# One kernel of attention, experts and feed-forward: the rare-case branch moves from the middle to the end, the mask limits come in one transfer, and TensorE gets more filler work at the start

## The chip, the cores and the metric

One NeuronCore of one Trainium2 chip. The time is that of one execution on the device, in microseconds. Before the change the median of 3 runs is 661.46 us (661.29 to 661.57). All inputs are fp32; the outputs are fp32 too.

## What is computed

Three layers in a row, on 2 x 768 = 1536 tokens of 512 features:

```
attention (8 heads of 64): each query sees the first n_sink = 4 keys and the last window = 128 keys
x   = softmax(q k^T / 8, masked) v                          # 1536 x 512
experts (8, of 512 -> 1024 -> 512), one per token:
e   = argmax(cos(x, expert_emb) / tau);  g = its softmax weight
x   = g * relu(x @ w1[e]) @ w2[e]
feed-forward (512 -> 1536 -> 512):
out = ((x @ w_a) * (x @ w_b)) @ w_out
```

n_sink, window and the split of tokens over experts are data: the kernel must be right for any values, and is laid out for the likely ones.

## The kernel before

Every large product is made of three TensorE products of rounded parts (hi x hi, lo x hi, hi x lo), so each operand is first split into `hi` (a cast on ScalarE, ACT) and `lo` (a difference on VectorE, DVE). Each engine runs its instructions in the order in which they are written (`manual_schedule`); semaphores keep the dependencies.

**Attention.** 12 blocks of 128 queries, four steps each (`g` counts them), software-pipelined: in step g TensorE makes the transposes of step g-2 (`p_t`), the score products of step g (`sc_mm`), the value products of step g-3 (`pv`) and some products that prepare the choice of expert (`back`). DVE adds the mask and takes the maximum, ACT makes the exponentials. The masks are built on DVE by `early_masks` from `ctli`, which holds n_sink and window for each partition and is filled by two small DMAs on the queue of SyncE (SP), between the first and the second halves of the first q and k blocks. `warm_pe(n)` puts n transposes of the identity, of no use for the result, on TensorE: 15 before the loop and `WARMG[g]` at the end of step g.

**Experts.** Tokens are gathered by expert and worked off in single tiles and pairs of tiles, out of a list `seq` of 81 items; the position in it is `i`. Beside it `side_gen` makes, three small steps an item, the tables for putting tokens back in order: `cidx`, the row of `y_d` that each token of the last stage reads, and `cide`, the same for the first four tiles, limited to the rows that are written early. At fixed items the last stage is prepared: `load_conv` loads its weights (SP queue), `conv_abs`, `conv_b0`, `conv_b1` and `conv_step` unpack and split them, `gather_y` gathers rows of `y_d` (POOL), `y_t` and `y_s` transpose and split them. The expert results go to DRAM through ACT (`y_out`) and SP.

**The covering path.** The plan has room for the likely spread of tokens. `cnt` counts what doesn't fit, or says that the mask limits are unlikely ones. All engines read it into a register (L1473) and branch (L1475): if it is zero, which it is here, the whole body is skipped; else the missing rows are computed slowly, and `y_d` is rewritten. Behind the branch the feed-forward stage begins.

**Feed-forward.** Three groups (`gi`) of 512 tokens, in each 12 slices (`f`) of 128 hidden features. `ab_mms` makes 24 products (`pp`), `g_split` multiplies the two halves and splits the product (ACT, DVE, ACT, DVE), `out_mms` adds 12 products to `po` one slice later. In the first group the weights of slices 2 to 11 are still unpacked on the way, two `conv_step` a slice. At the end of a group `done` scales the four result tiles and POOL writes them to `out` by indirect DMA.

Of the kernel before, what the change touches and what calls it, by code (L numbers as in the profile page):

```python
# [20 lines left out]
P = 128  # L21
# [42 lines left out]
WARMG = [6, 3, 4, 1]  # L64
# [38 lines left out]
TINY = 2.0 ** -15 * 1.125  # L103

# [19 lines left out]
def tile_kernel(ctx, tc, q, k, v, n_sink, window, emb, tau, w1, w2, wc, out, dbg=None):  # L124
# [62 lines left out]
    tt = pc.tile([E, 1], F32, name="tt")  # L187
    q0, k0 = new_q(0, 0), new_k(0, 0)
    for a in (0, W2):
        ld(q0, q, 0, 0, a, a + W2)  # L190
        ld(k0, k, 0, 0, a, a + W2)
        if a == 0:
            nc.sync.dma_start(ctli[:, 0:2], n_sink.bitcast(I32).partition_broadcast(P))
            nc.sync.dma_start(ctli[:, 2:4], window.bitcast(I32).partition_broadcast(P))
# [976 lines left out]
    fe = pool(ctx, "fe", side="right")  # L1171

    def side_gen(w_, pl, psp, tag):
# [172 lines left out]
        V.tensor_copy(cide, cpos[:, 0:4])  # L1346
        G.tensor_scalar(g, g, 1.0 / GSC, None, op0=ALU.mult)
# [16 lines left out]
    wres = {}  # L1364

    raw2, sq2 = {}, {}
# [3 lines left out]
    def load_conv(m):  # L1370
        if m >= NH:
            return
        r = raw2[m] = fe.tile([P, HW, 2], I32, tag="raw", name="raw2", bufs=3)
        nc.sync.dma_start(r.rearrange("p n c -> p (n c)"), wc32[m])

    def conv_abs(m):
        if m < NH:
            sq2[m] = fe.tile([P, HW], F32, tag="sq", name="sq", bufs=2)
            nc.scalar.activation(sq2[m], raw2[m][:, :, 1].bitcast(F32), AF.Abs)  # L1379

    def conv_b0(m):
        if m < NH:
            b, t = sq2[m], sq2[m].bitcast(I32)
            nc.vector.tensor_scalar(b, b, TINY, None, op0=ALU.max)  # L1384
            nc.vector.tensor_scalar(t, t, 5, 2, op0=ALU.logical_shift_left, op1=ALU.logical_shift_right)

    def conv_b1(m):
        if m < NH:
            r, t = raw2.pop(m), sq2[m].bitcast(I32)
            nc.vector.scalar_tensor_tensor(t, r[:, :, 0], 29, t, op0=ALU.logical_shift_right, op1=ALU.bitwise_or)  # L1390
            nc.vector.scalar_tensor_tensor(t, r[:, :, 1], -1073741824, t, op0=ALU.bitwise_and, op1=ALU.bitwise_or)  # L1391

    def conv_step(m, wpool):
        f, h = divmod(m, 2)
        if h == 0:
            wres[f] = (wpool.tile([P, CW], F32R, name=f"wh{f}"), wpool.tile([P, CW], F32R, name=f"wl{f}"))
        wh, wl = (t[:, h * HW:(h + 1) * HW] for t in wres[f])
        sq = sq2.pop(m)
        nc.scalar.copy(wh, sq)
        conv_b0(m + 1)  # L1400
        nc.vector.tensor_tensor(out=wl, in0=sq, in1=wh, op=ALU.subtract)  # L1401
        conv_abs(m + 2)
        conv_b1(m + 1)
        load_conv(m + 4)

    xh2 = fe.tile([P, NP, TG], F32R, name="xh2")
    xl2 = fe.tile([P, NP, TG], F32R, name="xl2")
    ygs = {}

    def gather_y(u, w=None, rows=None):  # L1410
        ygs[u] = w.tile([P, DM], F32, tag="ygn", name="ygn", bufs=4) if w else fe.tile([P, DM], F32, tag="yg", name="yg", bufs=3)
        early = u < 4 and w is None
        nc.gpsimd.indirect_dma_start(out=ygs[u], out_offset=None, in_=y_d[0:rows or (YR0 if early else YR1), :],  # L1413
                                     in_offset=bass.IndirectOffsetOnAxis(ap=(cide if early else cidx)[:, u:u + 1], axis=0))

    def y_t(u, psp, tag):
        yp = psp.tile([P, NP, P], F32, tag=tag, name="yp2")
        for kc in range(NP):
            nc.tensor.transpose(yp[:, kc, :], ygs[u][:, kc * P:(kc + 1) * P], ident)  # L1419
        return yp  # L1420

    def y_s(u, yp):
        tt = u % 4
        ts_ = slice(tt * P, (tt + 1) * P)
        nc.scalar.copy(xh2[:, :, ts_], yp)
        nc.vector.tensor_tensor(out=xl2[:, :, ts_], in0=yp, in1=xh2[:, :, ts_], op=ALU.subtract)
# [46 lines left out]
    ns_v = nc.values_load(cnt[0:1, 0:1], min_val=0, max_val=4 * int(GENF))  # L1473
    mst.close()
    with tc.If(ns_v > 0):  # L1475
# [97 lines left out]
        with ExitStack() as gs:  # L1573
            xw = pool(gs, "xw3")
            xps = pool(gs, "xps3", space=PSUM)
            for u in range(NU):
                gather_y(u, xw, NBLK * P)
                nc.sync.dma_start(y2_d[u * P:(u + 1) * P, :], ygs[u])
            for u in range(NU):
                yc = xw.tile([P, DM], F32, tag="ygn", name="yc", bufs=4)  # L1580
                nc.sync.dma_start(yc, y2_d[u * P:(u + 1) * P, :])
                nc.sync.dma_start(y_d[u * P:(u + 1) * P, :], yc)
            nc.vector.tensor_copy(cidx, tok)
            for u in range(4):
                gather_y(u, xw, YR1)
                y_s(u, y_t(u, xps, "a"))

    f1 = pool(ctx, "f1")
    f2 = pool(ctx, "f2", bufs=2, side="right")
    fpa = pool(ctx, "fpa", bufs=2, space=PSUM)  # L1590
    fpo = pool(ctx, "fpo", space=PSUM)

    def ab_mms(f):
        wh, wl = wres[f]
        ab = []
        for n in range(2):
            pp = fpa.tile([P, TG], F32, tag="ab"[n], name="pp")
            for kc in range(NP):
                ws = slice(n * 512 + kc * P, n * 512 + (kc + 1) * P)
                nc.tensor.matmul(pp, lhsT=wh[:, ws], rhs=xh2[:, kc, :], start=(kc == 0), stop=False)  # L1600
                nc.tensor.matmul(pp, lhsT=wh[:, ws], rhs=xl2[:, kc, :], start=False, stop=False)  # L1601
                nc.tensor.matmul(pp, lhsT=wl[:, ws], rhs=xh2[:, kc, :], start=False, stop=(kc == NP - 1))  # L1602
            ab.append(pp)
        return ab

    def g_split(f, ab, el):
        asb = f2.tile([P, TG], F32, tag="asb", name="asb", bufs=1)
        nc.scalar.copy(asb, ab[0])  # L1608
        nc.vector.tensor_tensor(out=asb, in0=ab[1], in1=asb, op=ALU.mult)  # L1609
        gh = f2.tile([P, TG], F32R, tag="gh", name="gh", bufs=2)  # L1610
        gl = f2.tile([P, TG], F32R, tag="gl", name="gl", bufs=2)
        nc.scalar.copy(gh, asb)  # L1612
        EL[el].tensor_tensor(out=gl, in0=asb, in1=gh, op=ALU.subtract)  # L1613
        return f, gh, gl

    def out_mms(po, f, gh, gl, done=None, tts=range(4)):
        wh, wl = wres[f]
        for tt in tts:
            ts_ = slice(tt * P, (tt + 1) * P)
            nc.tensor.matmul(po[tt], lhsT=gh[:, ts_], rhs=wh[:, 1024:CW], start=(f == 0), stop=False, skip_group_check=True)  # L1620
            nc.tensor.matmul(po[tt], lhsT=gh[:, ts_], rhs=wl[:, 1024:CW], start=False, stop=False, skip_group_check=True)  # L1621
            nc.tensor.matmul(po[tt], lhsT=gl[:, ts_], rhs=wh[:, 1024:CW], start=False, stop=(f == NF - 1), skip_group_check=True)  # L1622
            if done is not None:
                done(tt)

    NG = NT // TG
    outs = []
    pend = None
    tail = []
    for gi in range(NG):  # L1630
        po = [fpo.tile([P, DM], F32, tag=f"po{tt}", name=f"po{tt}") for tt in range(4)]
        for f in range(NF):
            ab = ab_mms(f)
            more = gi == 0 and f + NF0 < NF
            if more:
                conv_step(2 * (f + NF0), f1)
            cur = g_split(f, ab, 'V')
            if more:
                conv_step(2 * (f + NF0) + 1, f1)
            u0 = 4 * (gi + 1)  # L1640
            if f == NF - 2 and gi + 1 < NG:
                for tt in range(3):
                    gather_y(u0 + tt)
            if f == NF - 1 and gi + 1 < NG:
                yps = [y_t(u0 + tt, fpa, "ab"[tt]) for tt in range(2)]
                gather_y(u0 + 3)
                for tt in range(2):
                    y_s(u0 + tt, yps[tt])
            if pend is not None:
                if gi == NG - 1 and f == NF - 1:  # L1650
                    out_mms(*pend, tts=range(3))
                    tail.append(pend)
                else:
                    out_mms(*pend)
            pend = (po, *cur)
        if gi + 1 < NG:
            yps = [y_t(u0 + tt, fpa, "ab"[tt - 2]) for tt in range(2, 4)]

        def done(tt, gi=gi, po=po):
            os_ = fe.tile([P, DM], F32, tag="yg", name="os_", bufs=3)  # L1660
            u = gi * 4 + tt
# [63 lines left out]
```

## Time and profile before

| | |
|---|---|
| median of 3 runs | 661.46 us (661.29 to 661.57) |
| the profiled execution, whole | 659.85 us |
| its span, first to last instruction | 658.0 us |
| mean granted TensorE clock | 0.977 |
| attention, experts, feed-forward, about | 0 to 125, 125 to 329, 335 to 654 us |

All rows are from one profiled execution. PE is TensorE's products, PEld its weight loads, DVE VectorE, ACT ScalarE, POOL GpSimd, SP SyncE; a q behind a name means the sequencer of the engine, with its register, branch and semaphore instructions. L12 is line 12 of the kernel. A product's duration includes its way through the array, so products in a row overlap; their pace is the distance of their starts. The granted clock is a share of full speed: 1.00 is 2.4 GHz, 0.50 is 1.2 GHz.

### The profile page before, as it was taken

What the parts mean: (1) busy time and instruction counts of PE and PEld (TensorE: products, weight loads), DVE (VectorE), ACT (ScalarE), POOL (GpSimd) and SP (SyncE); (2) the same over time, 40 slices, a digit from 0 to 9 for tenths busy, and PEclk for the clock granted to TensorE, in tenths of its full rate; (3) what the DMA queues carried; (4) which work ended last, traced back from release to release, by engine and by line L of the source; (5) the groups of instructions that cost most, each with busy time, mean ns of one, the idle gap of its engine ahead of it and who ended that gap; (6) DMA issues with size and microseconds to landing.
All of it is one profiled execution on the core that took longest, in us unless ns stands there. A gap on an engine that the chain in (4) does not pass through costs nothing. (4 is left out here: it accounts for less than half of the span.)

```text
span 658.0 us, 10420 instructions
## 1 busy us (share of the span) xinstructions
PE 628.6 (96%) x3665; PEld 515.4 (78%) x3665; DVE 396.4 (60%) x910; ACT 304.8 (46%) x581; POOL 122.2 (19%) x269
## 2 busy tenths in 40 slices
PE   8999999889999999998969999999999999999995
PEld 5777777779998989887858767678888888888884
DVE  5688878998888766798839999943111113111111
ACT  4678777667575657667524444422111113111111
POOL 7243345481042211020010000004000003000002
PEclk7699999989999999999979999999999999999999
DMA  4244325323787887587253454203000002000001
GB/s 144 85 160 130 130 81 191 147 76 134 254 289 273 269 280 267 180 304 253 86 177 134 154 186 150 96 17 114 0 1 0 1 0 81 0 1 1 0 1 64
DMA packets 25967, 80.77 MB, mean 123 GB/s; under 512 B 3560, under 2 KB 4072, under 8 KB 25904
## 3 DMA queue, kind: packets, MB, share of 16 engines
q1 hardware_dynamic: 22560, 69.23, 31.5%
q0 software_dynamic: 3344, 10.77, 4.8%
q8 instruction: 31, 0.51, 0.3%
q14 instruction: 32, 0.26, 0.1%
HBM read 81.82 MB, written 10.75 MB: 141 GB/s over the span
## 5 line engine op out<-in xcount | busy, mean ns | idle before, releaser
L1600 PE MATMUL pp<-xh,wh 128*128 128x512 f32 x288 | 114.5, 398 | 5.7 <-DVEq L1475 5.7
L1609 DVE TENSOR_TENSOR asb<-pp,asb 128x512 f32<-128x512 f32 x36 | 24.8, 689 | 151.5 <-PE pp L1602 151.5
L1601 PE MATMUL pp<-xl,wh 128*128 128x512 f32 x288 | 114.9, 399 | 0.0
L1602 PE MATMUL pp<-xh,wl 128*128 128x512 f32 x288 | 114.6, 398 | 0.0
L603 DVE TENSOR_TENSOR lo<-raw,hi 128x1024 fp32r<-128x1024 f32 x80 | 96.1, 1228 | 7.9 <-ACT hi L595 6.2
L595 ACT CAST hi<-raw 128x1024 fp32r<-128x1024 f32 x87 | 88.0, 1050 | 7.8 <-PE hp L708 4.1
L1600 PEld LDWEIGHTS pp<-xh,wh 128*128 128x128 f32 x288 | 54.7, 190 | 19.4 <-ACTq L1475 6.2
L1601 PEld LDWEIGHTS pp<-xl,wh 128*128 128x128 f32 x288 | 54.8, 190 | 13.1
L1602 PEld LDWEIGHTS pp<-xh,wl 128*128 128x128 f32 x288 | 54.8, 190 | 12.9
L1612 ACT CAST gh<-asb 128x512 fp32r<-128x512 f32 x36 | 22.3, 620 | 90.2 <-DVE asb L1609 87.4
L1608 ACT COPY asb<-pp 128x512 f32<-128x512 f32 x36 | 21.0, 583 | 89.6 <-PE pp L1602 89.5
L1620 PE MATMUL po<-wh,gh 128*128 128x512 f32 x144 | 57.9, 402 | 3.9 <-ACT gh L1612 3.9
L477 ACT ACTIVATE p<-st,mn 128x260 f32<-128x260 f32 (+1 forms) x96 | 46.6, 487 | 29.2 <-DVE mn L474 22.8
L1622 PE MATMUL po<-wh,gl 128*128 128x512 f32 x144 | 57.6, 400 | 0.0
L1621 PE MATMUL po<-wl,gh 128*128 128x512 f32 x144 | 56.8, 394 | 0.0
L1413 POOL DMA_INDIRECT yg<-y_d,cidx x8 | 8.3, 1040 | 215.6 <-PE yp L1419 187.3
L780 PE MATMUL hT<-pxh,hi 128*128 128x256 f32 x160 | 45.5, 285 | 0.0
L782 PE MATMUL hT<-pxh,lo 128*128 128x256 f32 x160 | 44.7, 280 | 0.0
L781 PE MATMUL hT<-pxl,hi 128*128 128x256 f32 x160 | 44.7, 279 | 0.0
L474 DVE CUSTOM_DVE_ANT_0 st<-sc,m 128x260 f32<-128x260 f32 (+1 forms) x96 | 35.0, 399 | 10.4 <-PE sc L465 5.1
L1379 ACT ACTIVATE sq<-raw 128x768 f32<-128x768 f32 x24 | 22.1, 923 | 39.4 <-DVE wl L1401 39.4
L1613 DVE TENSOR_TENSOR gl<-asb,gh 128x512 fp32r<-128x512 f32 x36 | 24.9, 692 | 24.8 <-ACT gh L1612 24.8
(344 smaller groups left out, 1335.1 us busy)
## 6 DMA issues: line engine op xcount, KB each, us to landing
raw<-in_moe_w_dram SPq DMA_DIRECT2D x88, 512.0 KB
raw<-in_moe_w_dram SPq DMA_DIRECT2D x24, 768.0 KB
y_d<-ys SPq DMA_DIRECT2D x16, 256.0 KB
vt<-in_v_dram SPq DMA_DIRECT2D x12, 256.0 KB
x_d<-xl SPq DMA_DIRECT2D x12, 256.0 KB
qt<-in_q_dram SPq DMA_DIRECT2D x11, 256.0 KB
kt<-in_k_dram SPq DMA_DIRECT2D x10, 256.0 KB
qt<-in_q_dram SPq DMA_DIRECT2D x2, 128.0 KB
```

The source lines that it names most:

```text
L477: nc.scalar.activation(p[:, j, 0:W], st[:, 0:W], AF.Exp, bias=z['mn'][:, h:h + 1], scale=-1.0, accum_out=z['sm'][:, h:h + 1])
L595: ER = {'A': lambda o, i: nc.scalar.copy(o, i), 'V': lambda o, i: nc.vector.tensor_copy(o, i), 'P': lambda o, i: nc.gpsimd.tensor_copy(o, i)}
L603: EL[elo].tensor_tensor(out=lo, in0=raws[g], in1=hi, op=ALU.subtract)
L780: nc.tensor.matmul(hT[:, c, :], lhsT=hi[:, ws], rhs=z['xh'][:, kc, :], start=(c == 0 and kc == 0), stop=False, skip_group_check=True)
L781: nc.tensor.matmul(hT[:, c, :], lhsT=hi[:, ws], rhs=z['xl'][:, kc, :], start=False, stop=False, skip_group_check=True)
L782: nc.tensor.matmul(hT[:, c, :], lhsT=lo[:, ws], rhs=z['xh'][:, kc, :], start=False, stop=(kc == NP - 1), skip_group_check=True)
L1600: nc.tensor.matmul(pp, lhsT=wh[:, ws], rhs=xh2[:, kc, :], start=(kc == 0), stop=False)
L1601: nc.tensor.matmul(pp, lhsT=wh[:, ws], rhs=xl2[:, kc, :], start=False, stop=False)
L1602: nc.tensor.matmul(pp, lhsT=wl[:, ws], rhs=xh2[:, kc, :], start=False, stop=(kc == NP - 1))
L1620: nc.tensor.matmul(po[tt], lhsT=gh[:, ts_], rhs=wh[:, 1024:CW], start=(f == 0), stop=False, skip_group_check=True)
L1621: nc.tensor.matmul(po[tt], lhsT=gh[:, ts_], rhs=wl[:, 1024:CW], start=False, stop=False, skip_group_check=True)
L1622: nc.tensor.matmul(po[tt], lhsT=gl[:, ts_], rhs=wh[:, 1024:CW], start=False, stop=(f == NF - 1), skip_group_check=True)
```

## The change

- The branch and its body go behind the feed-forward stage. The stage is now the function `ffn_run`; it runs once without a condition, right behind the experts, on whatever `y_d` then holds. If `cnt` says so, the covering path at the end computes the missing rows and runs the whole stage again with its own buffers (`slow`).
- The register is read in the last group, slice 2, on all engines, and a hint for the branch (its target is likely taken) is placed there.
- All gathers of the normal pass use limited indices: `cidc`, two more small DVE operations in `side_gen`, one step later. In the covering path the detour over `y2_d` goes.
- n_sink and window are one input `limits` of two numbers, loaded by one DMA from ACT's queue, ahead of everything else there. The two DMAs on SP's queue go.
- `WARMG` goes from 6, 3, 4, 1 fillers in steps 0 to 3 (14) to 8, 7, 8, 2, 4, 4, 0, 0, 4, 4 in steps 0 to 9 (41).

Moved code that stays the same is left out here.

```diff
-WARMG = [6, 3, 4, 1]
+WARMG = [8, 7, 8, 2, 4, 4, 0, 0, 4, 4]
...
+    nc.scalar.dma_start(ctli, lim.bitcast(I32).partition_broadcast(P))
     q0, k0 = new_q(0, 0), new_k(0, 0)
     for a in (0, W2):
         ld(q0, q, 0, 0, a, a + W2)
         ld(k0, k, 0, 0, a, a + W2)
-        if a == 0:
-            nc.sync.dma_start(ctli[:, 0:2], n_sink.bitcast(I32).partition_broadcast(P))
-            nc.sync.dma_start(ctli[:, 2:4], window.bitcast(I32).partition_broadcast(P))
...
+    cidc = rt.tile([P, NU], I32, name="cidc")
+    fz = ctx.enter_context(ExitStack())
+    fe = pool(fz, "fe", side="right")
...
         V.tensor_copy(cide, cpos[:, 0:4])
+        yield
+        V.tensor_scalar(cpos[:, 4:NU], cpos[:, 4:NU], 0.0, float(YR1 - 1), op0=ALU.max, op1=ALU.min)
+        V.tensor_copy(cidc, cpos)
...
+        def gather_y(u):
+            ygs[u] = fe.tile([P, DM], F32, tag="yg", name="yg", bufs=3)
+            n, ix = (NBLK * P, cidx) if slow else (YR0, cide) if u < 4 else (YR1, cidc)
+            nc.gpsimd.indirect_dma_start(out=ygs[u], out_offset=None, in_=y_d[0:n, :], in_offset=bass.IndirectOffsetOnAxis(ap=ix[:, u:u + 1], axis=0))
...
-    ns_v = nc.values_load(cnt[0:1, 0:1], min_val=0, max_val=4 * int(GENF))
     mst.close()
-    with tc.If(ns_v > 0):
+
+    def ffn_run(z, stack, tag):
+        f1 = pool(stack, "f1" + tag)
+        f2 = pool(stack, "f2" + tag, bufs=2, side="right")
+        fpa = pool(stack, "fpa" + tag, bufs=2, space=PSUM)
+        fpo = pool(stack, "fpo" + tag, space=PSUM)
...
+                ab = ab_mms(f)
+                if not slow and (gi, f) == (NG - 1, 2):
+                    ns.append(nc.values_load(cnt[0:1, 0:1], min_val=0, max_val=4 * int(GENF)))
+                    tc.mark_branch_hint_location("cover", "LikelyTaken")
...
+    ns = []
+    ffn_run(ff, fz, "")
+    fz.close()
+    ns_v = ns[0]
+
+    with tc.If(ns_v > 0, label="cover"):
...
-            for u in range(NU):
-                gather_y(u, xw, NBLK * P)
-                nc.sync.dma_start(y2_d[u * P:(u + 1) * P, :], ygs[u])
...
+            ffn_run(ffn_parts(pool(gs, "fes", side="right"), True), gs, "s")
```

## Rows read from the trace of the kernel before

**Rows 1.** The page, busy time, share of the span and instructions of each engine.

```profile
PE 628.6 (96%) x3665; PEld 515.4 (78%) x3665; DVE 396.4 (60%) x910; ACT 304.8 (46%) x581; POOL 122.2 (19%) x269
```

**Rows 2.** Windows: stretch, length, busy us of each engine, granted clock, DMA share, GB/s.

```profile
3.00:3.50 0.50, 0.50 (x4) 0.50 (x3) 0.00 (x0) 0.00 (x0) 0.50 (x1) 1.00 0.08 7
...
10.00:15.00 5.00, 4.85 (x23) 3.10 (x24) 4.77 (x24) 3.99 (x17) 2.99 (x11) 0.50 0.20 48
...
26.50:27.00 0.50, 0.50 (x4) 0.19 (x4) 0.09 (x1) 0.02 (x1) 0.00 (x0) 0.68 0.00 0
...
330.00:335.00 5.00, 0.20 (x1) 0.23 (x2) 0.00 (x0) 0.00 (x0) 0.00 (x0) 0.90 0.68 218
335.00:340.00 5.00, 5.00 (x12) 3.90 (x13) 2.49 (x4) 1.17 (x2) 2.79 (x3) 0.50 0.21 72
...
400.00:410.00 10.00, 9.35 (x40) 6.95 (x39) 9.14 (x13) 4.94 (x8) 0.00 (x0) 1.00 0.54 174
```

**Rows 3.** Timeline around the branch: start, duration, engine, instruction, idle before and releaser.

```profile
328.66 0.40 PE L802 MATMUL yp<-lo,hh 128*128 128x512 f32 x1
334.80 0.77 PE L1600 MATMUL pp<-xh,wh 128*128 128x512 f32 x1 [5.74 <-DVEq L1475]
...
342.94 0.39 PE L1602 MATMUL pp<-xh,wl 128*128 128x512 f32 x1
...
327.64 1.28 DVE L1426 TENSOR_TENSOR xl<-yp,xh 128x512 fp32r<-128x512 f32 x2
337.33 0.60 DVE L1384 TENSOR_SCALAR sq<-sq 128x768 f32<-128x768 f32 x1 [8.40 <-issue]
...
343.44 0.69 DVE L1609 TENSOR_TENSOR asb<-pp,asb 128x512 f32<-128x512 f32 x1 [1.94 <-PE pp L1602]
...
329.09 0.58 ACT L595 COPY ys<-yp 128x512 f32<-128x512 f32 x1 [0.81 <-PE yp L802]
```

**Rows 4.** Line 1475, the branch: count, shortest/median/longest ns, first to last start.

```profile
L1475 POOLq EVENT_SEMAPHORE  x6: 17/30/43, 311.4 to 314.5; - x6
...
L1475 DVEq EVENT_SEMAPHORE  x2: 21/21/21, 334.6 to 334.7; - x2
L1475 POOLq COMPARE_BRANCH  x1: 58/58/58, 308.8 to 308.8; - x1
L1475 POOLq INC_SWDGE_SEM  x1: 660/660/660, 314.6 to 314.6; - x1
L1475 PEldq COMPARE_BRANCH  x1: 3532/3532/3532, 325.3 to 325.3; - x1
L1475 DVEq COMPARE_BRANCH  x1: 72/72/72, 328.4 to 328.4; - x1
```

**Rows 5.** The end: the last output transfer, and POOL's drains (line 1721).

```profile
652.62 0.97 POOL L1667 DMA_INDIRECT out_dram<-os__11394,ctok  x1 [0.22 <-ACT os__11394 L1663]
...
L1721 POOLq DRAIN  x3: 46/115/4799, 652.4 to 657.8; - x3
```

**Rows 6.** Timeline of the first steps (DVE, then PE).

```profile
5.90 0.21 DVE L222 CAST ctl<-ctli 128x4 f32<-128x4 int32 x1 [5.04 <-DMA ctli<-in_window_dram]
...
8.26 0.70 PE L459 MATMUL sc<-kf,qt 64*128 64x128 f32 x4 [1.41 <-DVE mn L474]
...
14.67 0.59 PE L465 MATMUL sc<-kh,qh 64*128 64x260 f32 x2
...
18.52 1.12 PE L490 MATMUL tp<-ident,p 128*128 128x128 f32 x4
...
26.82 0.39 PE L465 MATMUL sc<-kh,qh 64*128 64x260 f32 x2
...
28.55 0.60 PE L490 MATMUL tp<-ident,p 128*128 128x128 f32 x4
...
30.82 0.39 PE L465 MATMUL sc<-kh,qh 64*128 64x260 f32 x2
...
39.84 0.39 PE L465 MATMUL sc<-kh,qh 64*128 64x260 f32 x2
```

## What I predict, and why

> **What bounds the kernel now.** I read the page first: TensorE (PE) is busy for 96% of the span [rows 1], so what can be won is time in which it stands still, runs at half its clock, or waits in its queue's order for a slower engine. The windows say where that is [rows 2]. At the start the granted clock is 0.50 from about 10 us until it comes back at about 26.7. From 330 to 335 PE does next to nothing, and from 335 to 340 it works at 0.50. From there to the end of the first feed-forward group DVE is the bound: in 400 to 410 it is busy for 9.14 of 10 us, and PE has gaps.
>
> The timeline around the branch shows how the hole is made [rows 3]. PE's last expert product starts at 328.66, the first feed-forward product at 334.80, after 5.74 us idle that ended when DVE was through line 1475. The branch's own rows tell why [rows 4]: DVE's compare is done at 328.5, its next instruction comes at 334.6, 6.1 us later, though there is nothing to compute. PE's compare lasts 3.53 us; POOL has 2.5 us between its compare and the next instruction, and 6.4 us until its last one of that line is over. All engines take the branch, and whoever comes through last releases the stage.
>
> **The branch leaves the middle.** What must be there for the first feed-forward product is early: the first two slices' weights and tiles 0 to 3 of the tokens, whose last split on DVE ends at 328.92 [rows 3]. What remains is the accumulator. The new PSUM buffers take over those of the experts, and counting the expert accumulators in order, I take the first one to be that which ACT empties last, 329.09 to 329.67 [rows 3]. So PE starts at about 329.8 in place of 334.8: 5.0 us. I take it that a stop of under 1 us leaves the clock up, so the 24 products of slice 0 go at the pace of 400 to 410, 40 in 9.35 us, 0.234 us each: 5.4 us from the first to the last start in place of 8.14 (334.80 to 342.94). That is 2.75 us more, **-7.75 us** in all at `asb`, the DVE product that closes slice 0 (343.44 now, 335.7 then). If the buffer is free at once, PE starts at 329.06 and it is -8.5; if a second release of the same length comes in between, -7.1.
>
> Is DVE ready? What it does between the branch and `asb` lasts 343.44 - 1.94 - 337.33 = 4.17 us [rows 3] and can start at 328.9, so it is through at 333.1, 2.6 us early; its load issues move up with it. After `asb` the same chain runs as before, DVE-bound, so the shift is kept through the group and then by PE through the others.
>
> **The register in the last group.** In the middle PE's sequencer came to its compare at 325.3, while products queued before it went on until 329.06: the whole 3.53 us lay beside them [rows 3, 4]. The read within slice 2 of the last group is covered in the same way, and ACT, DVE, POOL and SP have idle time there. The hint is not in the trace: between nothing and 0.66 us, the longest of the small sequencer instructions of the branch [rows 4]; I take nothing, as it too is covered. Without cover the PE part would cost up to its 3.53. The two new small DVE steps are nearest to the cast of 0.21 us [rows 6]: 0.4 us, and I take nothing, since they stand long before `cidc` is read and PE has queued products beside them.
>
> **The branch at the end.** POOL is last there: its final output transfer starts at 652.62; its sequencer was free at 652.4, and the drain that waits for it ends at 657.2 [rows 5]. If the branch costs what it cost in the middle, 6.4 us counted from 652.4, it is over at 658.8, 1.6 us behind the drain. If the hint removes the 2.5 us before the first instruction at the target, it is over at 656.3, hidden. If it can only start behind the drain, all 6.4 us are added. The other engines come earlier: I take **+0.5**, between 0 and 6.4, because the nearest row (POOL's own) says that most of it fits beside the drain.
>
> Here the Trainium skill speaks against the change. "Runtime: NRT & Kernel Launch", section "Instruction fetch mechanics", says that a taken branch to a target that isn't loaded must first fetch it, and stalls; no sentence of it frees a branch with a hint. By that rule the 2.5 us of POOL's row come back at the end, and the sum would be 1.1 us higher. The trace agrees on the stall itself (2.5 to 6.1 us).
>
> **The mask limits.** `ctl` waits until 5.90 for the second of two loads, and PE has its second score products 2.36 us later, at 8.26, after 1.41 us idle [rows 6]. Between 3.0 and 3.5 the DMA engines are almost idle (share 0.08) [rows 2], although in SP's order the second halves of q and k and all later loads stand behind these two small ones: it is they that hold up the queue. With one load, first on ACT's queue, the masks can be ready once the first scores are, so DVE starts earlier; it is what counts here (busy 4.77 of 5 us in 10 to 15 [rows 2]). The bounds are nothing and 2.4 us (`ctl` at 3.5, the end of that idle stretch, in place of 5.90). I take **-1.5**, about PE's idle time, since that is how far the second scores can come forward.
>
> A rule differs: by "DMA: Bandwidth & Descriptors", section "Issuing engines are not separate DMA queues", another issuing engine saves only issue time, as all transfers share the same DMA engines. By that the -1.5 would be about 0. No run here shows which it is.
>
> **The fillers and the clock.** The clock fell after the idle 1.41 us before 8.26 and the thin stretch around it. The change closes it: earlier masks, and 23 in place of 13 fillers in steps 0 to 2. I think that PE then keeps 1.00. Four steps at half clock, from 14.67 to 26.82, took 12.15 us; four at full clock, 30.82 to 39.84, took 9.02 [rows 6]. That is **-3.1**, already with the limits of DVE in it. If it stays at half, it is 0; if the next two steps gain too, up to -4.
>
> Seventeen more fillers stand from step 3 on. Four such transposes last 0.60 us at full clock and 1.12 at half [rows 6]: at most 0.15 us each, 2.6 us. PE waits for DVE and ACT in a step for some part, so a third of it is paid: **+0.8**, between 0 and 2.6. At half clock all would be paid, 17 x 0.28 = +4.8.
>
> **The sum.** -7.75 + 0.5 - 1.5 - 3.1 + 0.8 = -11.05. The profiled execution took 659.85 us, so 648.8 in its terms. The median of the timed runs is 661.46, 1.61 above it; against that I predict **650.4 us**.
>
> **Rivals.** *The clock falls all the same.* Two waits are left to DVE and ACT in steps 3 to 8, and the granted clock did not come back for 17 us though PE had no long idle. Then the fillers cost 4.8 and the clock gives nothing: -7.75 + 0.5 - 1.5 + 4.8 = -3.95, 657.5; a fall for half the time gives about 654. Chance 0.22. *The end pays the branch.* The full 6.4 us stand behind the drain: 650.4 + 5.9 = 656.3; with the fetch alone, 651.5. For it: each engine paid in the middle; against it: POOL's drain and the hint. Chance 0.12. *The limits land no earlier*, because the small load is slow on any queue: the mask term goes, 651.9. For it: two such loads kept the engines almost idle; against it: there is one in place of two, with nothing before it [rows 2]. Chance 0.10. (This is what the DMA page of the Trainium skill would have.) *Slower:* the fetches at the end wait for one another and for the output data on the same DMA engines: 2.5 + 3.5 + 6.1 us of the three rows in turn, and POOL's 3.9 us of joining behind, 16.0 us [rows 4] in place of 0.5, gives 665.9. It decides from some 11 us on. Against it: in the middle they overlapped, and DVE and PE reach the end before POOL. Chance 0.04. Nothing else in the profile offers that much.
>
> **The numbers.** My forecast, clock kept and end hidden: 0.52, own range 647.5 to 652.5. For 8 in 10 I take 647 to 657: below it only all good ends together (-8.5, -2.4, -4, neither fillers nor end paid: 646.6), above it the cold clock's worst and the slower case. 0.2% is what can be told from no change here: 660.1 to 662.8. All cases but the last are below that, so faster 0.94, same 0.02, slower 0.04.
>
> **What would show it.** Right: PE idle under 1 us between the experts and the feed-forward, at 1.00 throughout; `asb` of slice 0 some 7.7 us earlier against the last expert product; `ctl` before 4.8; no 0.50 between 10 and 26; the last drain at most 1 us longer after the last output transfer. Wrong: a long wait of PE or ACT for an expert buffer, 0.50 in steps 3 to 9, event and branch rows behind the last drain. The prediction breaks most easily at the clock, on which 3.1 us and the price of the fillers hang.

## The result, and the profile after

The changed kernel took 651.02 us (median of 4 runs, 649.33 to 652.68), the kernel before on the same chip 661.38 us (4 runs, 660.43 to 661.57): a ratio of 0.9846, 95% interval 0.9819 to 0.9873. The forecast was 650.4 us, 0.6 us off. Its terms were not as good as its total. In the two profiled executions (659.85 and 651.05 us) the change is -8.8 us, where the sum said -11.05.

The page of the changed kernel, the answer to [rows 1]. Its profiled span is 649.2 us, in place of 658.0.

```profile
PE 621.7 (96%) x3692; PEld 510.9 (79%) x3692; DVE 398.1 (61%) x912; ACT 304.6 (47%) x581; POOL 120.6 (19%) x269
```

Windows of the changed kernel, columns as in [rows 2]:

```profile
15.00:20.00 5.00, 4.78 (x46) 3.33 (x43) 4.67 (x23) 4.34 (x16) 0.20 (x2) 1.00 0.69 234
...
138.00:140.00 2.00, 2.00 (x16) 2.00 (x15) 2.00 (x3) 0.03 (x1) 2.00 (x1) 0.80 0.53 164
140.00:142.00 2.00, 2.00 (x11) 2.00 (x11) 2.00 (x3) 1.53 (x2) 1.73 (x2) 0.50 0.26 98
142.00:144.00 2.00, 2.00 (x17) 2.00 (x17) 1.08 (x2) 0.88 (x2) 1.53 (x3) 0.85 0.60 150
...
325.00:330.00 5.00, 4.69 (x21) 3.88 (x22) 3.33 (x4) 2.50 (x4) 0.00 (x0) 1.00 0.80 254
```

The first steps run at 1.00 where they ran at 0.50, and so does the stretch from the experts into the feed-forward. What is left of a low clock stands at 139 to 143 us. The kernel before had the same there, behind a hole of its own (142 to 144):

```profile
142.00:144.00 2.00, 1.98 (x12) 1.99 (x13) 2.00 (x2) 0.52 (x1) 1.99 (x2) 0.72 0.40 113
```

So it hardly weighs in the comparison of these two executions; the experiments take it up.

The timeline of the changed kernel: first steps (DVE, then PE), the hole before 138, the way from experts to feed-forward (PE, ACT, DVE), and the last output transfer, against [rows 6], [rows 3] and [rows 5].

```profile
3.87 0.46 DVE L222 CAST ctl<-ctli 128x4 f32<-128x4 int32 x1 [3.02 <-DMA ctli<-in_limits_dram]
...
12.84 0.50 PE L465 MATMUL sc<-kh,qh 64*128 64x260 f32 x2 [0.49 <-DVE mn L474]
...
21.83 0.39 PE L465 MATMUL sc<-kh,qh 64*128 64x260 f32 x2
...
35.46 0.39 PE L465 MATMUL sc<-kh,qh 64*128 64x260 f32 x2
...
137.65 0.38 PE L708 MATMUL hp<-hi,xlo 128*128 128x256 f32 x1 [2.02 <-DVE xlo L672]
...
324.25 0.39 PE L802 MATMUL yp<-lo,hh 128*128 128x512 f32 x1
325.31 0.50 PE L1511 MATMUL pp<-xh,wh 128*128 128x512 f32 x1 [0.68 <-ACT ys L595]
...
324.68 0.59 ACT L595 COPY ys<-yp 128x512 f32<-128x512 f32 x1 [0.81 <-PE yp L802]
...
331.15 0.69 DVE L1520 TENSOR_TENSOR asb<-pp,asb 128x512 f32<-128x512 f32 x1 [2.31 <-PE pp L1513]
...
640.71 0.96 POOL L1581 DMA_INDIRECT out_dram<-os__7032,ctok  x1 [0.62 <-ACT os__7032 L1577]
```

Read against the rows of before, these give a ledger that closes:

- **Head.** The limits are cast at 3.87 in place of 5.90. Step 4 starts 1.83 us earlier (12.84 for 14.67), step 8 4.99 (21.83 for 26.82) and step 14 4.38 (35.46 for 39.84). The last expert product still stands 4.41 earlier (324.25 for 328.66). So -4.4 us is kept.
- **Experts to feed-forward.** From the last expert product to `asb` it is 6.90 us (331.15 - 324.25), where it was 14.78 (343.44 - 328.66): -7.9 us.
- **Last store.** `asb` is 12.29 earlier, the last output transfer only 11.91 (640.71 for 652.62). It waits 0.62 us for ACT where it waited 0.22: +0.4 us.
- **End.** From the start of the last transfer to the end of the span it is 8.49 us (649.2 - 640.71), where it was 5.38 (658.0 - 652.62): +3.1 us.

-4.4 - 7.9 + 0.4 + 3.1 = -8.8, which is the difference of the spans.

Line 1602 of the changed kernel is the branch at the end, line 1742 the closing drains (count, shortest/median/longest ns, first to last start):

```profile
L1602 POOLq EVENT_SEMAPHORE  x6: 17/30/43, 643.2 to 643.6; - x6
...
L1602 POOLq COMPARE_BRANCH  x1: 58/58/58, 640.5 to 640.5; - x1
L1602 POOLq INC_SWDGE_SEM  x1: 1060/1060/1060, 643.7 to 643.7; - x1
...
L1742 POOLq DRAIN  x3: 46/109/3586, 644.8 to 649.0; - x3
```

POOL compares at 640.5, has its next instruction at 643.2, is through its joining at 644.8, and only then starts a drain, which lasts 3.59 us (the joining is the row of event instructions and the INC_SWDGE_SEM behind the branch; the drains are among the last instructions of the program). Before, the long drain followed the last store at once: it ended at 657.2, and the store's own work at 653.59, so 3.6 us as well [rows 5].

### The profile page after: what moved, and what is told of

Its sections match the earlier page's. It is cut to its first block, busy times and chain, and to the rows that moved or that the text cites. A ratio compares the mean times of both kernels' runs of the same rounds, so it can differ in the third digit from the quotient of the medians.

```text
span 649.2 us, 10457 instructions
## 1 busy us (share of the span) xinstructions
PE 621.7 (96%) x3692; PEld 510.9 (79%) x3692; DVE 398.1 (61%) x912; ACT 304.6 (47%) x581; POOL 120.6 (19%) x269
## 4 chain that ended last, share of the span: by engine, by line
PE 56%; issue 19%; DVE 17%; ACT 4%; POOL 2%; DMA 1%; POOLq 0%; DVEq 0%; ACTq 0%
PE hp L708 5%; PE pp L1511 4%; PE pp L1512 4%; PE pp L1513 4%; PE ou L521 3%; PE hT L782 3%; PE hT L780 3%; PE hT L781 3%; PE yp L800 3%; PE yp L802 3%; PE yp L801 3%; DVE wl L1407 3%; DVE sq L1396 3%; PE sc L465 2%; PE tp L490 2%
## 5 line engine op out<-in xcount | busy, mean ns | idle before, releaser
L1512 PE MATMUL pp<-xl,wh 128*128 128x512 f32 x288 | 113.5, 394 | 0.0
L1419 POOL DMA_INDIRECT yg<-y_d,cidc x8 | 7.7, 962 | 208.0 <-PE yp L1424 181.4
```

## The experiments

Each kernel was timed beside the kernel before, in three groups with one chip to a group. The medians of before were 659.46 us (branch out, fall-through, old fillers, two loads) and 660.6 us in the other two groups.

**The covering path left out.** This kernel leaves out the branch and the whole covering path, which the inputs here never take.

```diff
-                    ns.append(nc.values_load(cnt[0:1, 0:1], min_val=0, max_val=4 * int(GENF)))
-                    tc.mark_branch_hint_location("cover", "LikelyTaken")
+                    pass
...
-    with tc.If(ns_v > 0, label="cover"):
```

> The changed kernel without the branch and the covering path at its end (left out: the case that rows don't fit the plan, which these inputs don't need). Theory A, the end pays for the branch on POOL: in the changed kernel POOL's compare comes at 640.5, its next instruction at 643.2, and its last drain starts only at 644.8, then lasts its 3.6 us; without the branch the drain starts right behind the last transfer (641.7), so 3.1 us less: ratio to before about 0.980, time about 648. The spread of the runs should shrink too, if it comes from that fetch. Rival B, the drain waits for the output data anyway: less than 0.5 us less, about 651.

It took 647.36 us (645.79 to 648.87), ratio 0.983 (0.9793 to 0.9867). Its last transfer, its drains, the window behind the hole, and the `asb` of slice 0:

```profile
638.60 0.97 POOL L1580 DMA_INDIRECT out_dram<-os__7018,ctok  x1 [0.19 <-issue]
```

```profile
L1639 POOLq DRAIN  x3: 46/104/4828, 638.3 to 643.7; - x3
```

```profile
140.00:142.00 2.00, 2.00 (x20) 2.00 (x19) 2.00 (x3) 1.67 (x3) 1.73 (x2) 1.00 0.27 104
```

```profile
329.62 0.69 DVE L1520 TENSOR_TENSOR asb<-pp,asb 128x512 f32<-128x512 f32 x1 [2.31 <-PE pp L1513]
```

The span ends at 644.0, 5.4 us behind the start of the last transfer, as before the change. So the branch at the end costs 3.1 us behind the start of the last transfer. In every profile with the branch at the end this stretch is 8.4 us or more, and 5.4 in the three without it (this one and the two kernels with the branch in the middle).

The last store's extra 0.4 us is gone too, and the rows say what it was. The fourth result tile takes the buffer of the first (there are three), so ACT's last product waits until the first store has landed. The time to landing of the first store, in the changed kernel and here:

```profile
out_dram<-os__7008,ctok POOLq DMA_INDIRECT x1, 3.2
```

```profile
out_dram<-os__6994,ctok POOLq DMA_INDIRECT x1, 2.7
```

In the changed kernel it lands at 639.64 and ACT goes on at 639.74; without the covering path the profile names that landing as what ACT waited for. From 630 us on that profile has 8 packets on the instruction queues, and this one has none. So the branch at the end costs this 0.4 us as well.

The remaining 1.7 us of this execution come from elsewhere, 1.5 of them there by `asb` (329.62 for 331.15): the clock did not fall behind the hole of 2.03 us at 137.66. The spread of the times did not shrink as expected (3.1 us, where the change has 3.4).

**The branch target falls through.** The covering path is asked to be the block that is jumped to, without the hint.

```diff
-                    tc.mark_branch_hint_location("cover", "LikelyTaken")
...
-    with tc.If(ns_v > 0, label="cover"):
+    with tc.If(ns_v > 0, label="cover", preferred_fallthrough_block=False):
```

> The changed kernel with the not-taken side laid out directly behind the compare, the covering body after it. Theory A1, what costs is the far jump over the body: POOL's 2.6 us between compare and next instruction go from there, but a jump to the last block is still to come behind the joining instructions, so the 2.6 us move and the time stays near 651. Rival A2, the fetch can run beside the joining instructions: 1 to 2.6 us less, 648.4 to 650. Rival B, the end isn't on the path: no change, and no gap moves.

654.2 us (653.42 to 655.82), ratio 0.9932 (0.991 to 0.9954): some 3 us slower than the change. The last transfer and its time to landing (us, last column), and the rows of the branch and of the drains:

```profile
640.20 0.97 POOL L1580 DMA_INDIRECT out_dram<-os__7032,ctok  x1 [0.19 <-POOLq L1601]
```

```profile
out_dram<-os__7032,ctok POOLq DMA_INDIRECT x1, 3.1
```

```profile
L1601 POOLq EVENT_SEMAPHORE  x6: 17/30/2984, 640.0 to 643.4; - x6
L1601 POOLq COMPARE_BRANCH  x2: 41/44/48, 639.9 to 644.6; - x2
...
L1741 POOLq DRAIN  x3: 46/109/3640, 647.1 to 651.4; - x3
```

The first compare now goes through at once (639.9, next instruction 640.0). But one event of the joining lasts 2.98 us, until the last store has landed (640.20 + 3.1 = 643.3). The jump out comes behind that, at 644.6, and the drain starts 2.5 us later still, at 647.1. The fetch was moved behind the joining, where nothing lies beside it. Theory A1 had the move right, but not the time (651). The first store lands in 2.7 us again, and the last one waits for nothing but its turn (0.19 us).

**A hint that is in the program.** In the trace of the changed kernel no engine runs a hint instruction, although one was asked for. Asked for GpSimd alone, one appears, 0.7 us from the start of POOL's stream:

```profile
L1742 POOLq BRANCH_PREFETCH_HINT  x1: 65/65/65, 0.7 to 0.7; - x1
```

```diff
-                    tc.mark_branch_hint_location("cover", "LikelyTaken")
+                    tc.mark_branch_hint_location("cover", "LikelyTaken", engines=[ET.Pool])
```

> The changed kernel, with the hint on the covering path's branch asked for on GpSimd alone, where the built program then holds one hint instruction, in the first instructions of GpSimd's stream (the changed kernel's main streams hold none). Theory G (a hint so early, 640 us ahead of its branch, keeps nothing fetched): GpSimd's gap from the compare to its next instruction stays at 2.6 us within 0.3, and the time is that of the changed kernel, 651 us. Rival H (the hint works from anywhere): the gap falls under 0.5 us and the time to 648.5 to 649 us.

651.76 us (650.86 to 652.64), ratio 0.988 (0.9847 to 0.9914). The last transfer, its time to landing, and the branch:

```profile
642.21 0.97 POOL L1581 DMA_INDIRECT out_dram<-os__7033,ctok  x1 [0.78 <-ACT os__7033 L1577]
```

```profile
out_dram<-os__7033,ctok POOLq DMA_INDIRECT x1, 2.7
```

```profile
L1602 POOLq EVENT_SEMAPHORE  x6: 17/30/2123, 642.5 to 645.0; - x6
L1602 POOLq COMPARE_BRANCH  x1: 64/64/64, 642.0 to 642.0; - x1
L1602 POOLq INC_SWDGE_SEM  x1: 1060/1060/1060, 645.1 to 645.1; - x1
```

Both expectations were half wrong. The gap behind POOL's compare is down from 2.7 to 0.5 us, and still the time is not shorter: the span ends at 650.6, 8.4 us behind the start of the last transfer (8.49 in the change). One event takes up the freed time, until 645.0, and the store lands at 642.21 + 2.7 = 644.9. In the changed kernel the same time to landing gives 640.71 + 2.7 = 643.4, beside a fetch that ends at 643.2:

```profile
out_dram<-os__7032,ctok POOLq DMA_INDIRECT x1, 2.7
```

There no event of the joining lasts over 0.043 us, so the fetch is what ends last, with the landing close behind it. Take the fetch away, as here, and the landing holds the joining, some 0.1 us sooner in all.

**The head.** The list of fillers of before:

```diff
-WARMG = [8, 7, 8, 2, 4, 4, 0, 0, 4, 4]
+WARMG = [6, 3, 4, 1]
```

> The changed kernel with the old number of fillers (6, 3, 4, 1). Theory C, the fillers keep the clock: the granted clock falls to 0.50 in the first 25 us again, the step that starts at 21.8 comes 2.5 to 3.5 us later: about 653 to 654. Rival D, the earlier masks alone keep it, by closing the idle time before the second scores: clock 1.00, and the fillers that are gone give back 0 to 1 us: 650 to 651.

653.83 us (652.04 to 655.08), ratio 0.9923 (0.9898 to 0.9948). Window and steps 8 and 14:

```profile
15.00:20.00 5.00, 5.00 (x30) 3.22 (x29) 3.73 (x19) 3.34 (x11) 0.02 (x1) 0.50 0.52 183
```

```profile
24.79 0.39 PE L465 MATMUL sc<-kh,qh 64*128 64x260 f32 x2
...
37.81 0.39 PE L465 MATMUL sc<-kh,qh 64*128 64x260 f32 x2
```

The clock goes to 0.50 again, though only from about 14 to 24 us (0.90, 0.50 and 0.57 in the three windows from 10 to 25), where it was about 10 to 27 before. Step 14 comes 2.35 us later (37.81 for 35.46). The fillers, clock and price together, are worth 2.3 us, which is what the forecast had (-3.1 + 0.8).

The limits in two loads on SP's queue, as before:

```diff
-    nc.scalar.dma_start(ctli, lim.bitcast(I32).partition_broadcast(P))
...
+        if a == 0:
+            nc.sync.dma_start(ctli[:, 0:2], lim[0:1].bitcast(I32).partition_broadcast(P))
+            nc.sync.dma_start(ctli[:, 2:4], lim[1:2].bitcast(I32).partition_broadcast(P))
```

> The changed kernel with the mask limits loaded as before, by two loads on SP's queue between the halves of q and k. Theory E, the two loads hold up the queue and the masks: the cast of the limits at about 5.9 in place of 3.9, 1.4 us of idle PE before the second scores again, 1.5 us more, about 652.5; if the clock falls too, 4 us more, about 655. Rival F, the load's place changes nothing but issue time: within 0.5 us of the changed kernel, cast before 4.8.

652.04 us (651.36 to 652.76), ratio 0.9899 (0.9864 to 0.9935). The cast (count, ns, first to last start), then the second score products and `asb` on the timeline:

```profile
L224 DVE CAST ctl<-ctli x1: 280/280/280, 6.0 to 6.0; 128x4 f32<-128x4 int32 x1
```

```profile
8.38 0.70 PE L461 MATMUL sc<-kf,qt 64*128 64x128 f32 x4 [0.90 <-DVE mn L476]
...
332.26 0.69 DVE L1522 TENSOR_TENSOR asb<-pp,asb 128x512 f32<-128x512 f32 x1 [2.31 <-PE pp L1515]
```

`asb` comes 1.1 us later than in the change. PE again stands idle before the second scores, for 0.90 us, and the clock still is at 1.00 in all windows from 5 to 30 us. With one load and the old fillers that idle time is gone and the clock falls, only later (at about 14 us in place of 10). So it is the fillers that keep the clock here; closing that wait alone put the fall off. The mean clocks of all runs agree: 0.980 to 0.987 with the old fillers, 0.990 to 0.993 here.

The one load, on SP's queue where the two had stood:

> The changed kernel, its one load of both mask limits moved from the head of ACT's queue to SP's queue, where the two loads of the kernel before stood, between the halves of the first q and k blocks. Theory I (what the change gained at the limits, 1.1 us, comes of the place at the head of an idle queue): the cast of the limits is later than 4.8 us and the time 0.6 to 1.1 us over that of the changed kernel. Rival J (it comes of one load in place of two): the cast is within 0.5 us of the 3.87 us of the changed kernel, and the time is that of the changed kernel within 0.4 us.

650.96 us (650.8 to 651.5), ratio 0.9864 (0.9836 to 0.9893), beside 650.87 for the change on the same chip. Its cast:

```profile
4.38 0.41 DVE L223 CAST ctl<-ctli 128x4 f32<-128x4 int32 x1 [3.52 <-DMA ctli<-in_limits_dram]
```

The cast is 0.5 us later than from ACT's queue, and the time is the same. So what counts is one transfer in place of two; the queue counts for nothing that can be measured in the time.

The whole head without the rest, that is the kernel before with the one load on ACT's queue and the new fillers:

> The kernel before, its branch between experts and feed-forward kept, with the changed kernel's head alone: the mask limits in one load on ACT's queue and the new list of fillers. Theory E (head and branch add up): the experts end 4.4 us earlier as in the changed kernel, the branch costs what it did (PE starts 5.7 us behind the last expert product, at a lower clock), and the time is the kernel before less 4.4 us, about 657 us, ratio 0.993. Rival (the earlier head moves the loads on SP's queue into a wait behind the branch, or is eaten before it): less than 2.5 us gained, 659 or more.

655.67 us (653.82 to 657.34), ratio 0.9933 (0.9912 to 0.9954): 4.9 us under before on its chip. The branch in the middle still stops PE:

```profile
331.99 0.77 PE L1598 MATMUL pp<-xh,wh 128*128 128x512 f32 x1 [5.79 <-DVEq L1473]
```

Head and branch add up, within the spread of the runs: 4.4 us was expected. The rest of the change then is worth 655.67 - 650.87 = 4.8 us, to be set beside 7.9 - 3.1 - 0.4 = 4.4 of the ledger.

**The clock behind the hole, and the levels.** Sixteen filler transposes put ahead of the product that waits for `xlo`:

```diff
     mm2_0()
+    wp2 = ps_t.tile([P, P], F32, tag="t", name="wp2")
+    for _ in range(16):
+        nc.tensor.transpose(wp2, ident, ident)
     lead(-1)
```

> The changed kernel, with 16 filler transposes on PE ahead of the first product of expert slot 1, where PE stood still from 135.6 to 137.65 us for the low half of the gathered rows (xlo). Theory D (the clock falls because of this hole, and whether it falls is what makes one run 1.5 us longer than another): the granted clock stays at 1.00 from 138 to 144 us, the product after the hole starts where it did (within 0.3 us), and the time is 1.5 us under that of the changed kernel, 649.5 us, with runs that differ by less than its 3.4 us. Rival (the clock falls there for another reason, or falls somewhere else instead): no change within 0.3 us, and a granted clock of 0.50 in 138 to 144 us, or in a later stretch. If the fillers are too many, the product after them starts up to 1 us later and eats most of it.

650.36 us (649.32 to 652.34), ratio 0.987 (0.9835 to 0.9906). In the profile the stretch has full clock:

```profile
140.00:142.00 2.00, 2.00 (x20) 2.00 (x19) 2.00 (x3) 1.67 (x3) 1.73 (x2) 1.00 0.30 109
```

The spread is hardly smaller (3.0 us for 3.4: three runs near 649.5, one at 651.1, two at 652.3), so the fall behind the hole is not its only source. That the fillers kept the clock here isn't shown by this one profile: the clock also stayed at 1.00 behind the unfilled hole without the covering path, and behind one of 2.02 us with the hint on POOL.

The change itself, once more:

> The changed kernel itself, on the chip of the two runs that follow. Theory D (one time of it is made up of how often the granted clock falls: in the first attention steps, and behind the pause at 137 us): the runs lie at levels about 1.5 us apart, some 649.3, 650.9 and 652.6, and of two runs the one with the higher mean clock is the shorter. Rival (a plain spread): values spread evenly, with no order by the clock.

650.87 us, ratio 0.9857 (0.983 to 0.9885); the runs are 649.45, 649.59, 650.75, 650.99, 651.21 and 652.52, which are the levels expected. The mean clocks (0.993, 0.993, 0.990, 0.990, 0.993, 0.988) put them in order with one exception, the run of 651.21. That one was profiled. It has the fall behind the hole (0.52 in 138 to 140); its mean is higher because the low clock behind PE's last product begins later (granted 1.00 in 641 to 643, where the first profile has 0.50). So a mean clock over the whole span also counts time in which PE has no work left.

The hole removed at its cause, by putting `xlo` ahead of two weight splits, and another buffer for the last store:

```diff
-    lead(-LEAD + L10)
     mm2_0()
+    lead(-LEAD + L10)
     lead(-1)
...
+                if u == NU - 1:
+                    os_ = fe.tile([P, HW], F32, tag="sq", name="sq", bufs=2)[:, 0:DM]
```

> The changed kernel with two edits: the second expert slot's low half (xlo) is put ahead of two weight splits on DVE's and ACT's streams, which fills the hole of 2.0 us without fillers; and the last store's buffer is another one, so that it does not wait for an earlier store. Theory D: the hole of 2.02 us is under 0.8 us, the clock stays at 1.00 from 138 to 144 us, and the last store waits for nothing but its product: 1.5 for the clock, 0.4 for the store, and up to 1.3 more for the hole itself, 647.8 to 649.1 us. Rival (DVE is the bound of this stretch, as it is busy without a pause from 130 to 142 us): the weights split 0.7 us later stop PE by as much within the next products, and only the clock and the store are kept, 649.1; if the pause moves and the clock falls there, 650.6.

649.1 us (648.47 to 650.2), ratio 0.9842 (0.9809 to 0.9875). PE's longest wait in that stretch and the last store:

```profile
137.93 0.39 PE L708 MATMUL hp<-lo,xh 128*128 128x256 f32 x1 [0.75 <-DVE lo L603]
...
639.17 0.97 POOL L1584 DMA_INDIRECT out_dram<-sq,ctok  x1 [0.19 <-issue]
```

```profile
out_dram<-sq,ctok POOLq DMA_INDIRECT x1, 3.2
```

```profile
L1605 POOLq EVENT_SEMAPHORE  x6: 17/30/864, 641.2 to 642.5; - x6
```

The hole is 0.75 us and the clock stays. The store no longer waits, but that buys little: it now takes 3.2 us to land, an event of the joining waits 0.86 us for it, and the span ends 8.9 us behind its start (648.1 - 639.17). This is the third run in which the long event of the joining ends with the landing (639.17 + 3.2 = 642.4).

The same with four fillers more in steps 3 and 4:

```diff
-WARMG = [8, 7, 8, 2, 4, 4, 0, 0, 4, 4]
+WARMG = [8, 7, 8, 4, 6, 4, 0, 0, 4, 4]
```

> The run with xlo first and the last store in a buffer of its own, and four fillers more in attention steps 3 and 4 (4 and 6 in place of 2 and 4), which each take 0.12 us of PE at the full clock. Theory K (the clock falls at 14 to 22 us in some runs because of PE's pauses of 0.26, 0.49 and 0.31 us between 11.6 and 13.7 us): fewer runs fall, the median is 646.5 to 648 us, under the 649.1 us of the run without them by 1 us or more. Rival L (the fillers stand where PE has work, and the pauses that matter are the two that wait for VectorE and GpSimd, which they can't fill): the same falls, and 0 to 0.5 us longer, 649 to 649.6 us.

648.87 us (648.61 to 650.85), ratio 0.984 (0.9813 to 0.9867). Four of its six runs are at 648.6 to 648.9, and the run without them had three of six at 648.5. Neither theory is decided by 0.2 us. It is the fourth run whose joining waits for the landing: one event lasts 0.53 us, to 641.39, and the store lands at 641.36. These two have the lowest medians of all that keep the covering path, about 1.8 us under the change, with ranges that overlap its range.

## Why the prediction was right, point by point

**The branch leaves the middle: right.** Forecast -7.75, measured -7.9. PE waits 0.68 us for ACT's last emptying, as counted (0.7), at full clock, and DVE stands ready 2.31 us before `asb` (forecast 2.6). The register read and the two small steps cost nothing that shows: from the first `asb` of the stage to the last it is 301.55 us, and 301.56 before.

**The branch at the end: the step that failed.** It was forecast at +0.5 and measured at +3.1, and with the last store's wait at +3.5. The prediction's own sign, a drain at most 1 us later, failed. The words were "most of it fits beside the drain", and nothing of it does. I had read the 4.80 us of [rows 5] as a wait for the last store, beside which a branch could run. The long drain starts only behind the joining, and takes 3.6 us even when the store has landed 1.4 us before it (643.4, drain at 644.8). In front of it stand, in the changed kernel, fetch and landing side by side (to 643.2 and 643.4), then about 0.3 us of events and 1.06 of INC_SWDGE_SEM. From the store's end at 641.67 to 644.8 that is 3.1 us, the measured price.

I had also left the hint open, as something that might take the fetch away. No engine of the changed kernel runs it. When POOL does, its fetch goes and the time stays, because the joining waits for the landing. "Runtime: NRT & Kernel Launch" of the Trainium skill, section "Instruction fetch mechanics", has a taken branch stall for its fetch. The trace agrees (2.7 us on POOL), and the run with POOL's fetch gone shows that removing this stall alone buys nothing.

**The last store: not foreseen.** It is +0.4 us, and belongs to the branch at the end. ACT's last product waits for the first store's buffer, and that store lands in 3.2 us in place of 2.7. With another buffer POOL's wait went and the last landing took as much longer. In the rival "Slower" I had let fetches and output data wait for one another; this 0.4 us is where the rows bear that out. That it is the fetches that slow the store is argued from their standing side by side: where none does, without the covering path and with the fall-through, the first store lands in 2.7 us.

**The head: 0.6 us too small.** Forecast -3.8 (-1.5 - 3.1 + 0.8), measured -4.4. One part undone at a time it is 1.1 for the limits and 2.3 for the fillers; the 1.0 us between their sum and 4.4 is lost only when both are undone, so either of them alone brings it. The terms of the forecast were added as if they were independent, and they aren't. The rival "the limits land no earlier" is refuted by the cast at 3.87. The Trainium skill, "DMA: Bandwidth & Descriptors", section "Issuing engines are not separate DMA queues", says that another issuing engine saves only the time of issuing, which is usually small. For the place of the load the trace agrees (650.96 beside 650.87); the gain that I set against that rule comes from there being one load.

**The clock.** It was kept in the head of the profiled run, as forecast, but not for the reason that I gave first. I had put the fall down to the 1.41 us of idle time before 8.26 and the thin stretch around it. With two loads most of that idle time is back (0.90 us) and the clock stays; with the old fillers it is gone and the clock falls, some 4 us later. Nor is the clock kept in every run: in three of the experiments that have these fillers (the hint on POOL, `xlo` first, and the head alone) the profile has 0.50, 0.66 and 0.78 in 15 to 20. The rival of a cold clock is real, in single runs, at 1.5 to 3 us by the levels of the times (649.4, 651, 652.5), and not at the 7 us that I gave it.

**The total.** The sum was 2.25 us too good (-11.05 for -8.8). I had then added 1.61 us, by which the profiled execution of before lay below its median, and the changed kernel's profiled execution lies at its median (651.05 and 651.02). The two errors nearly cancel, and that is luck: without it the forecast would be 2.25 us off, as the sum is.

## What to carry to other kernels

A branch around work that is never needed has its price where its last engine stands. Here that was, in the middle, PE's idle time and a low clock, and at the end three things in a row: the fetch or the landing of that engine's last transfer, whichever ends later, then the rest of the joining, then the drain. Before the cost of a step is hidden beside a closing drain, look at whether the drain can start earlier than that step ends. Compare kernels by several runs, and add a profile's distance from the median only if the kernel after it can be expected to have the same one.

## What the runs showed of the hardware that was not expected

The long drain on POOL takes 3.58 to 3.64 us in all thirteen profiles, counted from its own start or, where the last store still runs on POOL then (the kernel before, the covering path left out, the head alone), from the end of that. It takes as long with that store in flight as with the store landed. What it waits for is open.

A pause of PE of 2.0 us ahead of 138 us was followed by a granted clock of 0.50 in the profiled run of the change and not in that of the kernel without a covering path, with the same rows around it. The clock of the kernel before differs from run to run too: on one chip 5 of its 21 runs were at 656.1 to 656.4 us with a mean clock of 0.986 or 0.987, and the others mostly at 659 to 662 with 0.972 to 0.977. Set against the change's best runs (649.4), that is a gain of 6.7 us in place of 10. What decides in which runs the clock falls isn't shown by any of them.
